# Early attention units: outputs by single heads of 64 columns, scores by pairs of heads as 256 columns

## The chip, the cores and the metric

The kernel runs on one NeuronCore of one Trainium2 chip. Its time is the device time of one execution in microseconds (us). The engines are TensorE (PE in the profile, with its weight loads as PEld), VectorE (DVE), ScalarE (ACT), GpSimd (POOL) and SyncE (SP), which issues nearly all DMAs.

## The reference

A linear attention with a decaying state, followed by a feed-forward network with softplus.

```python
# q, k, v: (4, 8, 768, 64) float32
gamma = 1.0 - 2.0 ** (-5.0 - np.arange(H))
for t in range(S):
    state = gamma * state + k[:, :, t] (outer) v[:, :, t]        # (B, H, 64, 64)
    y[:, :, t] = (1 / sqrt(64)) * q[:, :, t] @ state
x = y.transpose(0, 2, 1, 3).reshape(3072, 512)
h = x @ w_in                                                      # (512, 2048), float64
g = np.maximum(h, 0) + np.log1p(np.exp(-np.abs(h)))
out = (g @ w_out).astype(np.float32)                              # (2048, 512), float64
```

## The kernel before

**Attention in units.** The attention is cut into 48 units: for each of the 4 batches, 6 chunks of C = 128 tokens, and for each chunk two halves `hf` of 4 heads. In a unit, the scores of a head are k times q over the 128 tokens of the chunk, masked to the lower triangle; the output of a head is v times the masked scores, plus (from the second chunk of a batch on, `if c`) the state times q; and the state grows by k times v. The decay is multiplied into q and v ahead of all that (`decay`, on GpSimd). Head dimension is D = 64, so two heads (a pair, index `j` = 0 or 1 in a unit, member `par` = 0 or 1) fill 128 partitions.

**Early units.** The first WHOLE = 12 units, which are the whole first batch, are computed with plain float32 matmuls. The other 36 units use float32r operands that are split into a high and a low part; the change does not touch those. For an early unit n, the parts are:

- `operands` (L224): four transposes on TensorE (L232) bring k and q of both pairs into one PSUM tile `tp`. The evacuation is L234 (ScalarE, the upper-left 64 partitions of k), L235 (VectorE, the other 64 partitions of k) and L236 (ScalarE, q whole). k goes into `kz`, in which each head has its own 128 columns with zeros on the partitions of the other head; q goes into `qs` with both heads of a pair on the 128 partitions. There is one `kz` for all units and one half of `qs` for even and one for odd units.
- `scores_whole` (L262): four matmuls of 128 columns, one for each head, with `kz` as weights and `qs` as moving operand (L267), one copy to SBUF on ScalarE (`a`, L268) and the mask on GpSimd (L260).
- `new_state` (L297): two matmuls k times v into PSUM (L307). `stack_state` (L315) copies the state to `stw`, a block-diagonal matrix of 128x128 for each pair (L323, one half on VectorE, one on ScalarE).
- `outputs` (L331): for each pair, one matmul of the 128x128 state with q of the pair (L342, if c), and two matmuls (L345), each with 128 weight columns: v of one head beside 64 columns of zeros. The zeros stand in the tile of v, `vns[i][:, :, 1, :]`, and are written once at the start (L524). All three add up in the same 128 columns of `yp`, whose 128 partitions are the two heads. The evacuation is one copy on ScalarE to `xh` (L346) and one subtraction on VectorE to `xl` (L347), each of 128x256: the high and the low part of the input of the feed-forward network.

A float32 matmul is two instructions in the profile, each with its own weight load: L345 shows 96 of each for 48 matmuls. The chunks 0 of the batch are units 0 and 1; so 10 of the 12 early units have `if c`.

**The network.** The weights arrive as float64 in 16 slices of 128 columns of d_ff (`load_weights`, L69 and L70 on SP's queue) and are turned into two float32r parts by ScalarE, VectorE and GpSimd (`convert_weights`, L85 to L98). `hidden` is three float32r matmuls for each piece (L436 to L438: high by high, low by high, high by low) into `hp`, `softplus_1` and `softplus_2` follow on VectorE, ScalarE and GpSimd (L444 to L453), and `second` is three more matmuls (L471 to L473).

**What sets the order.** `tick` places each part of a unit at a fixed offset from 16 times its number (L394 to L398), and the loop at L546 and `stages` (L588) interleave ticks with the first steps of the network. In these first steps a scheduler orders each engine's instructions; from `starts[2]` on (L617) TensorE's order is as written. Every engine works its own queue in order. Early units take their PSUM banks from `attention_bank` (L218): `tp`, `sc` and `yp` of successive units go by turns into two banks.

Pair p of chunks (256 tokens, 4 units) must have its `xh` and `xl` before `hidden` can start on it: units 0 and 2 for the first two pieces, units 1 and 3 for the others.

## Time and profile before

| what | value |
|---|---|
| median of 3 runs | 659.26 us (658.81 to 661.81) |
| profiled execution: its time | 661.7 us |
| profiled execution: its span, first to last instruction | 660.0 us |
| TensorE busy | 648.3 us, 98% of the span |
| VectorE, ScalarE, GpSimd busy | 411.9, 366.7, 319.3 us |
| granted TensorE clock, mean | 0.997 |
| last output matmul of an early unit (L345) starts | 110.5 us |

The profile is one execution. "Busy" of a matmul counts it from its start to a modelled end, so matmuls overlap in it; the pace at which TensorE works is the distance from one start to the next. Rows of a timeline give the start, the length and the number of instructions of a run of like ones. In a row of a line's instructions the three figures are the shortest, median and longest duration in ns.

### The profile page before, as it was taken

What the parts mean: (1) busy time and instruction counts of PE and PEld (TensorE: products, weight loads), DVE (VectorE), ACT (ScalarE), POOL (GpSimd) and SP (SyncE); (2) the same over time, 40 slices, a digit from 0 to 9 for tenths busy, and PEclk for the clock granted to TensorE, in tenths of its full rate; (3) what the DMA queues carried; (4) which work ended last, traced back from release to release, by engine and by line L of the source; (5) the groups of instructions that cost most, each with busy time, mean ns of one, the idle gap of its engine ahead of it and who ended that gap; (6) DMA issues with size and microseconds to landing.
All of it is one profiled execution on the core that took longest, in us unless ns stands there. A gap on an engine that the chain in (4) does not pass through costs nothing.

```text
span 660.0 us, 11777 instructions
## 1 busy us (share of the span) xinstructions
PE 648.3 (98%) x3762; PEld 555.2 (84%) x3762; DVE 411.9 (62%) x756; ACT 366.7 (56%) x799; POOL 319.3 (48%) x330
## 2 busy tenths in 40 slices
PE   7999999999999999999999999999999999999997
PEld 6898899888888888888888888888888888888896
DVE  5777888875685576576566665676677567522221
ACT  5867876656564555556565655565565555422221
POOL 5777758564445445444543464355345543332221
PEclk9999999999999999999999999999999999999999
DMA  9898573132223241131232132131222200000000
GB/s 241 227 260 239 161 195 86 37 76 41 42 62 62 39 96 21 26 84 35 40 84 37 35 92 35 17 82 29 46 61 48 41 19 33 0 1 33 0 33 32
DMA packets 153822, 46.69 MB, mean 71 GB/s; under 512 B 140448, under 2 KB 148640, under 8 KB 153760
## 3 DMA queue, kind: packets, MB, share of 16 engines
q1 hardware_dynamic: 153312, 45.93, 29.3%
q8 instruction: 29, 0.48, 0.3%
q14 instruction: 33, 0.27, 0.1%
q10 hardware_dynamic: 448, 0.01, 0.0%
HBM read 39.60 MB, written 6.29 MB: 70 GB/s over the span
## 4 chain that ended last, share of the span: by engine, by line
PE 92%; DMA 2%; ACT 2%; POOL 1%; issue 0%; DVE 0%; SPq 0%; POOLq 0%; ACTq 0%
PE hp L436 13%; PE hp L438 13%; PE acc L471 13%; PE acc L472 13%; PE hp L437 13%; PE acc L473 13%; PE yp L355 6%; PE sc L280 3%; PE stp L307 2%; DMA win<-in_moe_w_in_dram 2%; PE yp L345 1%; PE sc L267 1%; DMA vn<-in_v_dram 1%; PE yp L342 1%; PE tp L232 0%
## 5 line engine op out<-in xcount | busy, mean ns | idle before, releaser
L453 POOL TENSOR_TENSOR gl<-sp,gh 128x512 fp32r<-128x512 f32 x96 | 129.4, 1349 | 122.5 <-ACT gh L451 118.2
L436 PE MATMUL hp<-xh,winhl 128*128 128x512 f32 (+1 forms) x448 | 166.1, 371 | 1.0 <-DVE sp L449 0.5
L438 PE MATMUL hp<-xh,winhl 128*128 128x512 f32 (+1 forms) x448 | 162.0, 362 | 0.5 <-POOL winhl L98 0.5
L437 PE MATMUL hp<-xl,winhl 128*128 128x512 f32 (+1 forms) x448 | 161.7, 361 | 0.0
L445 ACT ACTIVATE sp<-sp 128x512 f32<-128x512 f32 x96 | 60.7, 632 | 167.7 <-DVE sp L444 167.6
L471 PE MATMUL acc<-wouthl,gh 128*128 128x512 f32 x384 | 151.0, 393 | 0.0
L472 PE MATMUL acc<-wouthl,gh 128*128 128x512 f32 x384 | 150.3, 391 | 0.0
L473 PE MATMUL acc<-wouthl,gl 128*128 128x512 f32 x384 | 149.0, 390 | 0.0
L444 DVE TENSOR_SCALAR sp<-hp 128x512 uint32<-128x512 uint32 x96 | 66.3, 690 | 84.8 <-PE hp L438 62.4
L438 PEld LDWEIGHTS hp<-xh,winhl 128*128 128x128 f32 x448 | 84.5, 189 | 14.3 <-POOL winhl L98 0.9
L436 PEld LDWEIGHTS hp<-xh,winhl 128*128 128x128 f32 x448 | 84.6, 189 | 12.3 <-PE yp L345 0.7
L437 PEld LDWEIGHTS hp<-xl,winhl 128*128 128x128 f32 x448 | 84.8, 189 | 11.2
L451 ACT CAST gh<-sp 128x512 fp32r<-128x512 f32 x96 | 59.7, 621 | 52.1 <-PE acc L472 40.0
L449 DVE SCALAR_TENSOR_TENSOR sp<-hp,sp 128x512 f32<-128x512 f32 x96 | 65.2, 680 | 33.7 <-ACT sp L445 33.2
L260 POOL TENSOR_SCALAR_AFFINE_SELECT a<-a 128x512 f32<-128x512 f32 x48 | 36.6, 762 | 101.6 <-DVE a L281 97.1
L473 PEld LDWEIGHTS acc<-wouthl,gl 128*128 128x128 f32 x384 | 71.8, 188 | 15.1
L471 PEld LDWEIGHTS acc<-wouthl,gh 128*128 128x128 f32 x384 | 72.1, 188 | 12.4
L472 PEld LDWEIGHTS acc<-wouthl,gh 128*128 128x128 f32 x384 | 72.4, 189 | 12.0
L213 POOL TENSOR_TENSOR vn<-vn,vtabs 128x256 f32<-128x256 f32 x48 | 29.8, 621 | 83.6 <-DMA vn<-in_v_dram 71.8
L281 DVE TENSOR_REDUCE a<-sc 128x256 f32<-128x512 f32 x72 | 49.3, 685 | 4.3 <-PE sc L280 3.5
L292 POOL TENSOR_TENSOR al<-a,ah 128x512 fp32r<-128x512 f32 x36 | 47.9, 1331 | 3.1 <-ACT ah L291 3.1
L329 DVE TENSOR_TENSOR st<-stp,st 64x128 fp32r<-64x128 f32 x60 | 17.3, 289 | 44.8 <-ACT st L327 44.2
(94 smaller groups left out, 919.3 us busy)
## 6 DMA issues: line engine op xcount, KB each, us to landing
win<-in_moe_w_in_dram SPq DMA_DIRECT2D x16, 512.0 KB, 4.9
wout<-in_moe_w_out_dram SPq DMA_DIRECT2D x16, 512.0 KB, 4.4
vn<-in_v_dram SPq DMA_DIRECT2D x48, 128.0 KB, 2.8
out_dram<-o SPq DMA_DIRECT2D x24, 256.0 KB, 2.1
vn<-in_k_dram SPq DMA_DIRECT2D x30, 128.0 KB, 2.4
kb<-in_k_dram SPq DMA_DIRECT2D x208, 16.0 KB, 1.7
qb<-in_q_dram SPq DMA_DIRECT2D x208, 16.0 KB, 1.7
qn<-in_q_dram SPq DMA_DIRECT2D x12, 128.0 KB, 4.9
```

What stands on the lines that cost most here:

```text
L281: summed[n] = nc.vector.tensor_reduce(sums[n][:, 2 * j:2 * j + 2, :], sc.rearrange("p h t c -> p h c t"), axis=mybir.AxisListType.X, op=AL ...
L436: nc.tensor.matmul(to, lhsT=wt[:, 0, d, :], rhs=xh[:, d], start=d == 0, stop=False)
L437: nc.tensor.matmul(to, lhsT=wt[:, 0, d, :], rhs=xl[:, d], start=False, stop=False)
L438: nc.tensor.matmul(to, lhsT=wt[:, 1, d, :], rhs=xh[:, d], start=False, stop=d == ND - 1)
L444: nc.vector.tensor_scalar(sp.bitcast(U32), hps[s].bitcast(U32), 0x80000000, None, op0=ALU.bitwise_or)
L445: nc.scalar.activation(sp, sp, AF.Softplus)
L449: nc.vector.scalar_tensor_tensor(g, hps.pop(s), 0.0, g, op0=ALU.max, op1=ALU.add)
L451: nc.scalar.copy(gh, g)
L453: nc.gpsimd.tensor_tensor(gl, sps.pop(s), gh.bitcast(F32), op=ALU.subtract)
L471: nc.tensor.matmul(to, lhsT=gh[:, k, ts], rhs=wt[:, 0], start=first, stop=False)
L472: nc.tensor.matmul(to, lhsT=gh[:, k, ts], rhs=wt[:, 1], start=False, stop=False)
L473: nc.tensor.matmul(to, lhsT=gl[:, k, ts], rhs=wt[:, 0], start=False, stop=last)
```

## The change

The early units get other operands and other shapes; nothing else is touched.

- k of a pair is kept whole (`kts`, 128 partitions, one half of the tile for even and one for odd units), and q of each head stands beside zeros (`qzs`, one tile for even and one for odd units). So the 64-partition copies L234 and L235 now bring q, and the 128-partition copy L236 brings k.
- Scores: two matmuls of 256 columns, one for each pair, with k of the pair as weights and q of both heads as moving operand.
- Outputs: for each head by itself a matmul of the state (64 of its columns, if c) and one of v (64 columns, no zeros beside it). `yp` is on 64 partitions with 512 columns. It is evacuated in two halves: copy and subtraction for the even heads to partitions 0 to 63, then copy and subtraction for the odd heads to partitions 64 to 127.
- At the start the zeros of v are no longer written (three memsets on VectorE), those of `kz` (two on GpSimd) become four: two on GpSimd, two on VectorE.

In the changed kernel the v matmul is L343 (L345 before), the cast L345 (L346), the subtraction L346 (L347), and the network's lines are lower by one (L435 for L436).

```diff
-    kz = attn.tile([P, 2, NJ, C], F32, name="kz", tag="vhl", bufs=2)
-    qs = attn.tile([P, 2, NJ, C], F32, name="qs", tag="vhl", bufs=2)
+    kts = attn.tile([P, 2, NJ, C], F32, name="kts", tag="ah")
+    qzs = [attn.tile([P, 2, NJ, C], F32, name=f"qz{i}", tag="vhl", bufs=2) for i in range(2)]
...
-            qt = qs[:, n % 2]
-            nc.scalar.copy(kz[lo, 0], tp[lo, 0])
-            nc.vector.tensor_copy(kz[up, 1], tp[up, 0])
-            nc.scalar.copy(qt, tp[:, 1])
-            live[n] = [qt, rest[0], vn]
+            qz = qzs[n % 2]
+            nc.scalar.copy(qz[lo, 0], tp[lo, 1])
+            nc.vector.tensor_copy(qz[up, 1], tp[up, 1])
+            nc.scalar.copy(kts[:, n % 2], tp[:, 0])
+            live[n] = [qz, rest[0], vn]
...
-        for h in range(HH):
-            nc.tensor.matmul(sc[:, h, :], lhsT=kz[:, h % 2, h // 2, :], rhs=kq[:, h // 2, :], start=True, stop=True)
+        for j in range(NJ):
+            nc.tensor.matmul(sc[:, 2 * j:2 * j + 2, :], lhsT=kts[:, n % 2, j, :], rhs=qz[:, :, j, :], start=True, stop=True)
...
-            yp = attention_bank(n, [P, NJ, C], "yp")
-            v0 = vns[n % 3].rearrange("p h t d -> p (h t) d")
-            for j in range(NJ):
+            yp = attention_bank(n, [D, 2, NJ, C], "yp")
+            for h in range(HH):
+                j, par = divmod(h, 2)
                 if c:
-                    nc.tensor.matmul(yp[:, j], lhsT=st[:, j, :], rhs=kq[:, j, :], start=True, stop=False)
-                for par in range(2):
-                    at = 2 * (2 * j + par) - par
-                    nc.tensor.matmul(yp[:, j], lhsT=v0[:, at:at + 2, :], rhs=a[:, 2 * j + par, :], start=c == 0 and par == 0, stop=par == 1)
-            nc.scalar.copy(xh, yp)
-            nc.vector.tensor_tensor(xl, yp, xh.bitcast(F32), op=ALU.subtract)
+                    nc.tensor.matmul(yp[:, par, j], lhsT=st[:, j, par * D:(par + 1) * D], rhs=kq[:, par, j, :], start=True, stop=False)
+                nc.tensor.matmul(yp[:, par, j], lhsT=vn[:, h, :], rhs=a[:, h, :], start=c == 0, stop=True)
+            for par, own, oth in sides:
+                nc.scalar.copy(xh[own], yp[:, par])
+                nc.vector.tensor_tensor(xl[own], yp[:, par], xh[own].bitcast(F32), op=ALU.subtract)
             return
...
-    for par, own, oth in sides:
-        nc.gpsimd.memset(kz[oth, par], 0.0)
+    for qz, engine in zip(qzs, (nc.gpsimd, nc.vector)):
+        for par, own, oth in sides:
+            engine.memset(qz[oth, par], 0.0)
...
-    for vn in vns:
-        nc.vector.memset(vn[:, :, 1, :], 0.0)
```

Two places of the built programs, before and after. First TensorE where unit 2 puts out its heads and the network begins. A number behind a name tells its allocation: `yp_277` (before) and `yp_275` (after) are the outputs of unit 2, `yp_335` of unit 3 in both, `sc_296` and `sc_298` the scores of unit 3, `hp` the first hidden piece. "x2" counts matmuls. Before:

```order
L345 MATMUL yp_277<-a_237,vn2_92 128x128 x2
L342 MATMUL yp_277<-qs_87,stw0_88 128x128
L345 MATMUL yp_277<-a_237,vn2_92 128x128 x2
L436 MATMUL hp_385<-xh_82,winhl_251 128x256
L267 MATMUL sc_296<-qs_87,kz_86 128x128 x4
L437 MATMUL hp_385<-xl_83,winhl_251 128x256
```

And after:

```order
L343 MATMUL yp_275<-a_237,vn2_93 64x128
L342 MATMUL yp_275<-qz0_87,stw0_89 64x128
L343 MATMUL yp_275<-a_237,vn2_93 64x128
L342 MATMUL yp_275<-qz0_87,stw0_89 64x128
L343 MATMUL yp_275<-a_237,vn2_93 64x128
L342 MATMUL yp_275<-qz0_87,stw0_89 64x128
L343 MATMUL yp_275<-a_237,vn2_93 64x128
L267 MATMUL sc_298<-qz1_88,kts_86 128x256 x2
L307 MATMUL stp_94<-vn0_91,kn_194 128x128 x2
L342 MATMUL yp_335<-qz1_88,stw1_90 64x128
L435 MATMUL hp_387<-xh_82,winhl_249 128x256
```

The eight output matmuls of unit 2 alternate between state and v, and the scores, the state and the first output matmul of unit 3 now stand ahead of the first hidden matmul. Then ScalarE's queue around the same evacuation (`xh<-yp`). Before:

```order
L346 CAST xh_82<-yp_277 128x2x128
L236 COPY qs_87<-tp_269 128x256
L85 ACTIVATE win_207<-win_207 128x512
L323 COPY stw0_88<-stp_93 64x2x64
L97 CAST wouthl_318<-w_314 128x512
```

And after:

```order
L345 CAST xh_82<-yp_275 64x2x128
L323 COPY stw0_89<-stp_94 64x2x64
L97 CAST wouthl_318<-w_314 128x512
L85 ACTIVATE wout_206<-wout_206 128x512
L268 COPY a_297<-sc_298 128x512
L345 CAST xh_82<-yp_275 64x2x128
```

The one cast of unit 2 has become two, and four instructions stand between them, the last of them the copy of unit 3's scores.

More of the change, by code (lines that the diff above doesn't have):

```diff
@@ L262, in scores_whole @@
     def scores_whole(n):
-        kq = live[n][0]
+        qz = live[n][0]
         a = attn.tile([P, HH, C], F32, name="a")
         sc = attention_bank(n, [P, HH, C], "sc")
-        for h in range(HH):
-            nc.tensor.matmul(sc[:, h, :], lhsT=kz[:, h % 2, h // 2, :], rhs=kq[:, h // 2, :], start=True, stop=True)
+        for j in range(NJ):
+            nc.tensor.matmul(sc[:, 2 * j:2 * j + 2, :], lhsT=kts[:, n % 2, j, :], rhs=qz[:, :, j, :], start=True, stop=True)
         nc.scalar.copy(a, sc)
```

## The prediction

> **What bounds the kernel now.** I began with the page: busy time of each engine, the 40 slices, and the chain that ended last.
>
> ```profile
> PE 648.3 (98%) x3762; PEld 555.2 (84%) x3762; DVE 411.9 (62%) x756; ACT 366.7 (56%) x799; POOL 319.3 (48%) x330
> ...
> PE   7999999999999999999999999999999999999997
> ...
> PE 92%; DMA 2%; ACT 2%; POOL 1%; issue 0%; DVE 0%; SPq 0%; POOLq 0%; ACTq 0%
> ```
>
> TensorE is busy in every slice and makes up 92% of the chain. Time that TensorE needs more or less is therefore time of the kernel, unless it falls where TensorE waits anyway. So the next view is the busy time in stretches of 30 us up to 120 us, since the early units end at 110.5 us. The columns are the length of the stretch, then PE, PEld, DVE, ACT and POOL busy, then the clock, the DMA share and GB/s.
>
> ```profile
> 0.00:30.00 30.00, 24.77 (x147) 21.63 (x148) 18.63 (x47) 19.40 (x41) 18.90 (x33) 0.94 0.91 238
> 30.00:60.00 30.00, 28.11 (x207) 25.90 (x206) 21.84 (x39) 23.92 (x51) 23.86 (x36) 1.00 0.86 234
> 60.00:90.00 30.00, 29.45 (x212) 27.51 (x211) 23.89 (x43) 23.22 (x46) 20.80 (x20) 1.00 0.66 192
> 90.00:120.00 30.00, 29.79 (x198) 27.16 (x198) 25.50 (x42) 20.57 (x44) 21.26 (x21) 1.00 0.45 113
> ```
>
> TensorE idles 5.2 us in the first stretch, 1.9 in the second, and 0.6 and 0.2 in the others. VectorE and ScalarE are busy 20 to 25 us of 30: loaded, but not the bound. What TensorE waits for after the start, in the view of waits from 15 to 125 us, is this (us in all, times, longest):
>
> ```profile
> PE yp L342 <- ACT a L268: 1.5, 2, 1.0
> PE stp L307 <- POOL vn L213: 0.8, 1, 0.8
> PE sc L267 <- ACT qs L236: 0.6, 1, 0.6
> ...
> PE hp L436 <- ACT xh L346: 0.5, 1, 0.5
> ```
>
> These are single waits of about 1 us or less. So the change must be priced first by the pace of the matmuls that it removes and adds, then by these waits.
>
> **The pace of the matmuls.** The distance between starts gives it. From TensorE's timeline at 109 us (outputs of the last early unit), at 99 us (scores) and at 92 us (transposes):
>
> ```profile
> 109.49 0.61 PE L345 MATMUL yp<-a,vn 128*128 128x128 f32 x4
> 109.94 0.39 PE L342 MATMUL yp<-qs,stw 128*128 128x128 f32 x2
> ```
> ```profile
> 99.75 0.28 PE L437 MATMUL hp<-xl,winhl 128*128 128x256 f32 x1
> 99.87 0.28 PE L438 MATMUL hp<-xh,winhl 128*128 128x256 f32 x1
> 99.99 1.06 PE L267 MATMUL sc<-qs,kz 128*128 128x128 f32 x8
> ```
> ```profile
> 92.58 0.38 PE L232 MATMUL tp<-ident,kn 128*128 128x128 f32 x2
> 92.80 0.38 PE L232 MATMUL tp<-ident,qn 128*128 128x128 f32 x2
> ```
>
> Four float32 instructions in 109.94 - 109.49 = 0.45 us: 112 ns each (128 weight columns, 128 moving columns). The hidden matmuls, float32r with 256 moving columns, come every 120 ns. The transposes come every 0.22 / 2 = 0.11 us, 110 ns. The third shape is that of the later units, 64 weight columns in float32r:
>
> ```profile
> 122.89 0.39 PE L473 MATMUL acc<-wouthl,gl 128*128 128x512 f32 x1
> 123.11 0.64 PE L355 MATMUL yp<-ah,vhl 128*64 128x128 f32 x8
> 123.59 0.40 PE L355 MATMUL yp<-al,vhl 128*64 128x128 f32 x4
> 123.83 0.45 PE L436 MATMUL hp<-xh,winhl 128*128 128x512 f32 x1
> 124.11 0.40 PE L437 MATMUL hp<-xl,winhl 128*128 128x512 f32 x1
> ```
>
> Eight in 0.48 us: 60 ns each. The step from L473 to L355 gives 0.22 to 0.23 us for 512 float32r columns. So float32r moves a column in about 0.45 ns: 128 in 60, 256 in 120, 512 in 230.
>
> The question on which the change turns is what sets the 112 ns of a float32 instruction: its weight load (128 columns), or its moving columns at half the rate of float32r. No row of before shows float32 with 64 weight columns or 256 moving ones. The weight loads' durations (shortest, median, longest) in the views of three lines bear on it:
>
> ```profile
> L345 PEld LDWEIGHTS yp<-a,vn x96: 186/192/192, 10.1 to 110.4; 128*128 128x128 f32 x96
> L355 PEld LDWEIGHTS yp<-ah,vhl x288: 134/134/135, 122.9 to 582.1; 128*64 128x64 f32 x144
> L232 PEld LDWEIGHTS tp<-ident,kn x24: 138/142/230, 4.3 to 92.6; 128*128 128x128 f32 x24
> ```
>
> Half the columns shorten the load from 192 to 134 ns. The transposes' load is nearly as short, 142 ns, yet their pace is 110 and not 60. Something other than the load holds them, and what they share with the float32 matmuls and not with L355 is a float32 moving operand of 128 columns. I take it that float32 moves at about 0.85 ns a column, so that fewer weight columns gain nothing. Lower bound of an output instruction with 64 weight columns: 60 ns (L355); upper: 112 ns (L345); I take 110, by the transposes. For 256 moving float32 columns: lower 120 ns (the hidden matmul), upper 230 ns (twice the columns at half rate, as 512 float32r columns); I take 222, twice 110 and a little.
>
> The Trainium skill, page "TensorE: Matmul & The Clock Gate", sections "LDWEIGHTS (loading the stationary operand)" and "Back-to-back issue gap", says that a load costs by its number of columns and a matmul by its moving columns, and makes no difference for float32. By that rule an output instruction would cost the 60 ns of L355 and the sum would be the gain of the first rival; that the load shrinks with its columns agrees (192 to 134 ns), that the rest follows does not, by the transposes' 110 ns.
>
> **The change part by part.**
>
> *Outputs, units 2 to 11.* Removed: 6 matmuls of two instructions, 12 x 112 = 1.344 us. Added: 8 matmuls, 16 x 110 = 1.760 us. That is +0.416 us for each of 10 units, +4.2 us (bounds: 16 x 60 gives -3.8, 16 x 112 gives +4.5). The cause is that the state's and v's products no longer share 128 output columns of the array. *Units 0 and 1:* 8 instructions of 112 become 8 of 110: nothing (at 60: -0.8 for both).
>
> *Scores, 12 units.* 8 x 112 = 0.896 us become 4 x 222 = 0.888: -0.1 us in all (bounds: 4 x 120 gives -5.0, 4 x 230 gives +0.3).
>
> *Operands.* The same three copies with k and q exchanged, the same shapes: nothing. That `kz` is doubled frees a wait that no row of TensorE shows (L236 is waited for as the last of three copies, not for its buffer), so I expect no gain.
>
> *Evacuation.* One cast and one subtraction become two each. A copy costs by its columns, not its partitions:
>
> ```profile
> L346 ACT CAST xh<-yp x12: 352/370/381, 11.8 to 112.2; 128x256 fp32r<-128x256 f32 x12
> ...
> L378 ACT COPY vn<-yp x14: 363/366/367, 125.0 to 203.1; 64x256 f32<-64x256 f32 x14
> ```
> ```profile
> L347 DVE TENSOR_TENSOR xl<-yp,xh x12: 385/410/427, 12.2 to 113.7; 128x256 fp32r<-128x256 f32 x12
> ```
> ```profile
> DVE kz L235 <- ACT kz L234: 6.3, 3, 3.5
> ```
>
> So ScalarE gets 12 x 0.37 = 4.4 us more and VectorE 12 x 0.41 = 4.9 us, over about 100 us in which they have 15 to 30% free: covered by TensorE as throughput. As latency it is at least 0.37 + 0.41 = 0.8 us more for each unit, because the two engines take turns on one bank, as they already do in the operands (in the view of all waits up to 125 us, VectorE's copy L235 idles for ScalarE's L234; the change gives the outputs the same form). Behind the second cast on ScalarE stand weight conversions, behind the second subtraction on VectorE likewise; and TensorE waits for `xh` and for the bank. In the orders above, the second cast of unit 2 comes after the copy of unit 3's scores, and the first hidden matmul after unit 3's first output matmul, which waits for the same bank. Before, TensorE waited there 0.5 us (L436, row above) and 1.0 at most on L342; the scores, state and output matmul that now stand between (about 1.4 us) cover most of the longer evacuation. Bounds for the waits over all units: -1 us (a wait of L342 or L267 falls out, rows above) to 12 x 0.8 = +9.6 us (each one lands on TensorE). I take +0.8, one evacuation of 12, since of 12 units before only one made L436 wait.
>
> *Memsets and start.* Three memsets on VectorE go, two come, all before TensorE's first transposes: nothing.
>
> *Switches between 64 and 128 weight columns.* The Trainium skill, page "TensorEngine Tiling (Array Packing)", section "Key Properties", says that changing the tiling mode drains TensorE, which speaks against this change. The rows at 122.89 to 124.11 show the switch: 0.22 us into L355, no more than between two matmuls of 512 columns, and on the way back 0.28 instead of 0.23, the 0.05 by which a 128-column load outlasts a 60 ns matmul. I price it at nothing, and at 110 ns a matmul covers that load too.
>
> *Sum:* +4.2 - 0.1 + 0.8 = +4.9 us. The profiled execution took 661.7 us, 1.7 over its span of 660.0 and 2.4 over the median of 659.26. It would become 666.6; on the median, 664.2 us.
>
> **The rivals.**
>
> *The weight load was the limit* (the other side: faster). If float32 columns move as fast as float32r, the sum is -3.8 - 0.8 - 5.0 = -9.6 us, with +0.8 for the evacuation -8.8: 650.5 us. For it: 112 ns is also what a 128-column load takes when nothing covers it (60 + 0.05 us at 123.83). Against it: the transposes. It decides at about 95 ns for 128 float32 columns: with p for that, outputs and scores sum to 272 p - 26.0 us (16 instructions in 10 units, 8 in 2, 4 of double length in 12; 26.0 is what they take before). 0.10.
>
> *The first waits absorb it.* Four of the ten units, 2 to 5, are put out by 42.1 us. The chain then runs over SP's queue and a weight DMA into a wait of TensorE (rows of the chain, and of TensorE's timeline):
>
> ```profile
> 41.62 0.46 PE yp L345 x4
> 42.08 0.13 SPq L178
> 42.34 6.54 DMA win<-in_moe_w_in_dram
> ```
> ```profile
> 49.47 0.28 PE L438 MATMUL hp<-xh,winhl 128*128 128x256 f32 x1
> 50.73 0.49 PE L342 MATMUL yp<-qs,stw 128*128 128x128 f32 x2 [0.98 <-ACT a L268]
> ```
>
> If that transfer starts no later, 4 x 0.416 = 1.7 us vanish in this wait, and with no new waits +2.4 us remain: about 661.7 us, from +0.5 to +3.3. Against it: by the chain the transfer is issued behind a load (L178) that waited for an output matmul, so it would start later too. 0.24.
>
> *The evacuation becomes the wait.* If the ping-pong on the bank costs half its bound, +4.8 instead of +0.8, the sum is +8.9: 668.2 us. For it: VectorE is busy up to 25.5 of 30 us in these stretches, and each half must pass through both queues. Against it: only one such wait before. 0.11.
>
> *Each switch drains.* Counted from the changed order, about 20 bursts of 64-column matmuls, two switches each, at the 0.16 us by which an L355's duration (0.64 - 7 x 0.06 = 0.22) exceeds its pace: +6.4, 670.6 us. Rows at 123 us speak against it. 0.02.
>
> **How the numbers follow.** My forecast, +3.3 to +6.5 us, has 0.53. A measurement can tell about 0.5%, 3.3 us. Faster than that is only the first rival: 0.10. Within it lies the second: 0.24. Slower: 0.53 + 0.11 + 0.02 = 0.66. The likeliest is 664.2 us. The range leaves out the first rival and the upper part of the third: 659.5 (the second at its lower end) to 669.0 us.
>
> **What would show it.** In the changed profile: L343 and L342 with weight loads near 134 ns but starts 108 to 112 ns apart (60 would mean the first rival); L267 starts 215 to 230 ns apart (120 would); the first matmul of the later units (L355, now L354) about 5 us later than 122.9 to 123.1; ScalarE and VectorE busy 4 to 5 us longer. A view of waits in which hidden matmuls wait for L345 or L346 for more than 3 us in all would be the third rival; a wait near 50 us that is shorter than 1 us with the L354 mark less than 3 us later, the second. If L354 begins earlier than before, the pace I took for float32 is wrong.

## The result, and the profile after

The changed kernel takes 669.29 us (median of 4 runs, 669.0 to 670.1), the kernel before 659.51 us beside it (4 runs, 658.81 to 661.81). The ratio is 1.0143 (95%: 1.0121 to 1.0166), so the change costs 9.8 us by the medians and 9.4 by the ratio. The direction was forecast, the size was twice the forecast's 4.9 us, and the time lies 0.3 us above the range. The profiled execution took 669.25 us, with a span of 667.5. (One of the four runs of e16 below took 2281 us and is left out of its figures.)

The page of the changed kernel, the same lines as shown of before:

```profile
PE 654.1 (98%) x3754; PEld 554.3 (83%) x3754; DVE 416.4 (62%) x767; ACT 370.8 (56%) x811; POOL 319.0 (48%) x330
...
PE 92%; ACT 2%; DVE 2%; DMA 1%; issue 0%; ACTq 0%; DVEq 0%
```

TensorE is busy 5.8 us longer (4.1 were counted), VectorE 4.5 and ScalarE 4.1 (4.9 and 4.4). TensorE's share of the chain is what it was; it doesn't show where 9 us came from. The first output matmuls of the later units do (TensorE's timeline):

```profile
130.46 0.39 PE L472 MATMUL acc<-wouthl,gl 128*128 128x512 f32 x1
130.68 0.64 PE L354 MATMUL yp<-ah,vhl 128*64 128x128 f32 x8
```

They begin at 130.68 instead of 123.11: 7.6 us are lost before that mark, and the span is 7.5 us longer. All of it lies in the early units. Busy time in the first stretches (columns as in the prediction):

```profile
0.00:30.00 30.00, 22.26 (x126) 17.61 (x127) 19.38 (x48) 20.07 (x43) 19.01 (x33) 1.00 0.91 238
30.00:60.00 30.00, 29.22 (x193) 25.12 (x192) 23.25 (x43) 25.04 (x53) 22.93 (x34) 1.00 0.86 247
```

TensorE idles 7.7 us in the first 30 us (5.2 before), and then less than before, 0.8 instead of 1.9. So most of the loss is not visible idle time. TensorE is busy for longer than the passes account for, and the timeline shows with what. The last early unit, after:

```profile
115.55 0.39 PE L472 MATMUL acc<-wouthl,gl 128*128 128x512 f32 x1
115.86 0.43 PE L342 MATMUL yp<-qz,stw 128*64 128x128 f32 x2
116.13 0.38 PE L343 MATMUL yp<-a,vn 128*64 128x128 f32 x2
...
117.44 0.38 PE L343 MATMUL yp<-a,vn 128*64 128x128 f32 x2
117.75 0.39 PE L435 MATMUL hp<-xh,winhl 128*128 128x256 f32 x1
117.98 0.28 PE L436 MATMUL hp<-xl,winhl 128*128 128x256 f32 x1
```

The same place of before (the passes between are in the prediction):

```profile
109.05 0.39 PE L473 MATMUL acc<-wouthl,gl 128*128 128x512 f32 x1
...
110.53 0.36 PE L436 MATMUL hp<-xh,winhl 128*128 128x256 f32 x1
110.73 0.28 PE L437 MATMUL hp<-xl,winhl 128*128 128x256 f32 x1
```

Take the time from the start of the network's pass ahead of the outputs to the start of the second one behind them. Before it is 1.68 us for 12 output passes, after it is 2.43 us for 16: 0.75 us more, where the prediction has 0.42. Inside the burst the pace is the forecast one: 12 passes from 116.13 to 117.44, 109 ns each. The rest stands at the ends. From L472 to L342 it is 0.31 us instead of 0.23, the first pair takes 0.27 instead of 0.22, the first network pass begins 0.31 us after the start of the last pair, and the second 0.23 us after the first: together 0.54, where before has 0.34. So going to 64 weight columns and back costs about 0.3 us in float32. Next the scores:

```profile
106.53 1.03 PE L267 MATMUL sc<-qz,kts 128*128 128x256 f32 x4
107.21 0.58 PE L470 MATMUL acc<-wouthl,gh 128*128 128x512 f32 x1
107.63 0.39 PE L471 MATMUL acc<-wouthl,gh 128*128 128x512 f32 x1
```

From 106.53 to 107.63, less 0.23 for the network's pass, are 0.87 us for four passes of 256 columns: 217 ns each, as forecast (222).

The other suspect is the evacuation. Who waits for the subtraction L346 in the changed kernel (us, times):

```profile
L346 DVE TENSOR_TENSOR xl<-yp,xh x24: 404/417/419, 11.8 to 120.6; 64x256 fp32r<-64x256 f32 x24
...
  ACT xh L345: 1.7, 2
  PE yp L342: 1.2, 1
  PE yp L343: 1.0, 1
```

Before, the same list was empty for L347: nobody waited for the subtraction. Now TensorE's next output matmuls wait 2.2 us for it, because their bank is read out later. An example is unit 1, whose matmuls start at 14.0 us in both kernels. Before, ScalarE and VectorE had:

```profile
15.21 0.37 ACT L346 CAST xh<-yp 128x256 fp32r<-128x256 f32 x1 [0.41 <-PE yp L345]
```
```profile
16.32 0.42 DVE L347 TENSOR_TENSOR xl<-yp,xh 128x256 fp32r<-128x256 f32 x1
```

After, ScalarE and then VectorE:

```profile
15.05 0.36 ACT L345 CAST xh<-yp 64x256 fp32r<-64x256 f32 x1 [0.21 <-PE yp L343]
...
16.03 0.69 ACT L85 ACTIVATE win<-win 128x512 f32<-128x512 f32 x1
16.61 0.62 ACT L97 CAST wouthl<-w 128x512 fp32r<-128x512 f32 x1
17.25 0.36 ACT L345 CAST xh<-yp 64x256 fp32r<-64x256 f32 x1
```
```profile
16.36 0.41 DVE L346 TENSOR_TENSOR xl<-yp,xh 64x256 fp32r<-64x256 f32 x1
16.70 0.69 DVE L93 TENSOR_SCALAR wp<-win 128x512 uint32<-128x512 uint32 x1
17.49 0.70 DVE L94 SCALAR_TENSOR_TENSOR wp<-win,wp 128x512 uint32<-128x512 uint32 x1
18.22 0.42 DVE L346 TENSOR_TENSOR xl<-yp,xh 64x256 fp32r<-64x256 f32 x1
```

Before, the bank was free at 16.74; after, at 18.64. The second half adds 0.78 us of its own and stands behind two weight conversions on each engine: 1.9 us in all. Unit 2's first output matmul then waits 1.2 us.

So there are two theories. **Switches and passes:** TensorE's own time grew, by 0.75 us in a unit whose outputs stand in one burst, as those of the last unit do. **Halves:** the evacuation in two pieces makes TensorE wait. The first is worth more than 10 x 0.75 = 7.5 us of TensorE's time: eight of the ten units are put out in two bursts (one pair of passes, then seven), and with units 0 and 1 the changed kernel has 20 bursts of 64 columns, so by this count it is 10 x 0.42 + 20 x 0.30 = 10.2 us. The second can't be priced from these two kernels. A third, that the queues of weight conversions are what sets the early time, came up on the way.

### The profile page after: what moved, and what is told of

Same layout as the page of the kernel before. It is cut to its first block, busy times and chain, and to the rows that moved or that the text cites. A ratio compares the mean times of both kernels' runs of the same rounds, so it can differ in the third digit from the quotient of the medians.

```text
span 667.5 us, 11791 instructions
## 1 busy us (share of the span) xinstructions
PE 654.1 (98%) x3754; PEld 554.3 (83%) x3754; DVE 416.4 (62%) x767; ACT 370.8 (56%) x811; POOL 319.0 (48%) x330
## 4 chain that ended last, share of the span: by engine, by line
PE 92%; ACT 2%; DVE 2%; DMA 1%; issue 0%; ACTq 0%; DVEq 0%
PE hp L435 13%; PE hp L436 13%; PE acc L470 13%; PE hp L437 13%; PE acc L471 13%; PE acc L472 13%; PE yp L354 6%; PE sc L280 3%; PE stp L307 2%; PE yp L343 1%; PE yp L342 1%; PE sc L267 1%; DMA wout<-in_moe_w_out_dram 1%; DVE wp L94 0%; DVE w L95 0%
## 5 line engine op out<-in xcount | busy, mean ns | idle before, releaser
L435 PE MATMUL hp<-xh,winhl 128*128 128x512 f32 (+1 forms) x448 | 165.9, 371 | 0.3 <-ACT wp L91 0.3
L436 PE MATMUL hp<-xl,winhl 128*128 128x512 f32 (+1 forms) x448 | 162.2, 362 | 0.0
L470 PE MATMUL acc<-wouthl,gh 128*128 128x512 f32 x384 | 151.4, 394 | 0.6 <-ACT gh L450 0.6
L471 PE MATMUL acc<-wouthl,gh 128*128 128x512 f32 x384 | 150.2, 391 | 0.0
L472 PE MATMUL acc<-wouthl,gl 128*128 128x512 f32 x384 | 149.0, 390 | 0.2 <-POOL gl L452 0.2
L435 PEld LDWEIGHTS hp<-xh,winhl 128*128 128x128 f32 x448 | 84.5, 189 | 12.4 <-ACT wp L91 0.5
L436 PEld LDWEIGHTS hp<-xl,winhl 128*128 128x128 f32 x448 | 84.8, 189 | 11.9 <-issue 0.7
L472 PEld LDWEIGHTS acc<-wouthl,gl 128*128 128x128 f32 x384 | 71.9, 188 | 15.7 <-POOL gl L452 0.4
L470 PEld LDWEIGHTS acc<-wouthl,gh 128*128 128x128 f32 x384 | 72.1, 188 | 13.3 <-ACT gh L450 0.8
L471 PEld LDWEIGHTS acc<-wouthl,gh 128*128 128x128 f32 x384 | 72.4, 189 | 12.1
```

The lines of the kernel that those rows point to most:

```text
L435: nc.tensor.matmul(to, lhsT=wt[:, 0, d, :], rhs=xh[:, d], start=d == 0, stop=False)
L436: nc.tensor.matmul(to, lhsT=wt[:, 0, d, :], rhs=xl[:, d], start=False, stop=False)
L470: nc.tensor.matmul(to, lhsT=gh[:, k, ts], rhs=wt[:, 0], start=first, stop=False)
L471: nc.tensor.matmul(to, lhsT=gh[:, k, ts], rhs=wt[:, 1], start=False, stop=False)
L472: nc.tensor.matmul(to, lhsT=gl[:, k, ts], rhs=wt[:, 0], start=False, stop=last)
```

## The experiments

Ratios are against the kernel before, run beside each (its medians 659.5 to 660.9 us). "Last unit" is the change of the last early unit's outputs against before, measured as above, times 10 units. "Bursts" counts the stretches of matmuls with 64 weight columns in the early units. "Busy" and "idle" are TensorE's in the profile up to the mark, the first output matmul of the later units; for before they are 115.2 and 7.9 us, and 115.1 and 6.8 in its second profile (e1).

| run | outputs | evacuation | last unit x 10, us | bursts | busy, idle, us | median, us | ratio (95%) |
|---|---|---|---|---|---|---|---|
| e3 | 64 columns, halves of the array side by side | one piece | -0.6 | 17 | 114.1, 7.1 | 660.43 | 1.0000 (0.9986 to 1.0013) |
| e8 | state 128, v 64 columns | one piece | +2.4 | 22 | 114.5, 8.0 | 660.96 | 1.0013 (1.0001 to 1.0024) |
| e5 | 16 passes of 128 columns | one piece | +4.5 | 0 | 117.0, 6.5 | 662.26 | 1.0023 (1.0011 to 1.0036) |
| e2 | as before | halves | 0 | 0 | 115.1, 12.0 | 667.08 | 1.0104 (1.0089 to 1.0119) |
| e6 | as e3 | halves | -0.6 | 19 | 116.7, 12.3 | 668.11 | 1.0111 (1.0088 to 1.0134) |
| e4 | as changed | halves, both casts first | +7.5 | 17 | 120.5, 8.9 | 668.87 | 1.0131 (1.0114 to 1.0148) |
| changed | 16 passes of 64 columns | halves | +7.5 | 20 | 121.0, 9.6 | 669.29 | 1.0143 (1.0121 to 1.0166) |

The last unit stands for all only where each unit is put out in one burst. Busy times compare only to about 2 us, since in some of these profiles the granted clock was lower for a while: 0.66 between 15 and 20 us in before, e1, e3 and e6, which is 1.7 us of TensorE's full pace, and 0.94 in one stretch of 30 us in e2 and e6, which is 1.8.

**e1, before once more, unchanged** (one run): how far two profiles of one kernel differ.

> The kernel before once more, for a second profiled execution. The one shown took 661.7 us, 2.2 over the median of 659.5. Both theories expect about 659.5 here, with the first output matmul of the later units (L355) at about 121 us instead of 123.1; then the change's cost up to that mark is near 9.8 us and not the 7.6 that the two profiles so far show, and some 6 of it are waits. If the mark stays at 123 with a time of 661 or more, the two profiles can be compared as they are.

661.98 us; the mark of the later units is at 121.99 us, against 123.11 in the first profile. By these two, one profile's mark is good to about 1 us.

**e2, only the halves, in the kernel before.**

```diff
-            nc.scalar.copy(xh, yp)
-            nc.vector.tensor_tensor(xl, yp, xh.bitcast(F32), op=ALU.subtract)
+            for par, own, oth in sides:
+                nc.scalar.copy(xh[own], yp[own])
+                nc.vector.tensor_tensor(xl[own], yp[own], xh[own].bitcast(F32), op=ALU.subtract)
```

> The kernel before with one edit: its evacuation in two halves of 64 partitions (cast, subtraction, cast, subtraction), no matmul touched. Theory E (the waits come from the evacuation in halves): 663 to 667 us, that is 4 to 7 over before. Theory O (the waits come from the new order and the new operands): within 2 us of before, 658 to 661.5.

667.08 us, 1.0104: 6.9 us without any change of a matmul. Busy time up to the mark (121.99 and 127.06 us), of e1 and then of e2:

```profile
0.00:121.90 121.90, 115.13 (x770) 104.72 (x771) 93.10 (x172) 88.57 (x180) 86.95 (x109) 0.99 0.72 192
```
```profile
0.00:127.00 127.00, 115.05 (x770) 104.29 (x771) 97.02 (x186) 94.37 (x193) 86.66 (x110) 0.99 0.69 185
```

TensorE has the same 770 instructions and the same 115.1 us of work, and idles 12.0 us instead of 6.8. What it waits for in e2, from 15 to 132 us:

```profile
PE yp L342 <- ACT a L268: 2.8, 3, 1.4
PE yp L342 <- DVE xl L348: 1.2, 1, 1.2
...
PE sc L280 <- DVE a L281: 1.1, 1, 1.1
PE sc L267 <- ACT qs L236: 1.1, 1, 1.1
```

Only one of these waits is for the evacuation itself. The three others shown, 5.0 us, are for copies on ScalarE and VectorE, in whose queues the second halves now stand; the rows left out, 2.8 us, are for GpSimd. So the price is spread over other work. TensorE's order is hardly another: in the traces, the number of network matmuls ahead of each unit's last output matmul differs from e1's by five at most.

**e3, changed kernel, but each head's outputs on its own partitions and one evacuation.**

```diff
-            yp = attention_bank(n, [D, 2, NJ, C], "yp")
+            yp = attention_bank(n, [P, NJ, C], "yp")
...
+                own = sides[par][1]
...
+                nc.tensor.matmul(yp[own, j], lhsT=vn[:, h, :], rhs=a[:, h, :], start=c == 0, stop=True)
+            nc.scalar.copy(xh, yp)
+            nc.vector.tensor_tensor(xl, yp, xh.bitcast(F32), op=ALU.subtract)
```

> The changed kernel with the outputs of odd heads written to partitions 64 to 127 of the bank, so that one cast and one subtraction evacuate a unit; the same matmuls otherwise. Theory E: only the matmul work of 3.6 us is left, 662 to 664.5 us. Theory O: 667 to 670 us. If TensorE runs matmuls of different column halves side by side, starts less than 100 ns apart would show it and the time would be under 661 us.

660.43 us, 1.0000. The same two places of TensorE's timeline:

```profile
107.48 0.39 PE L472 MATMUL acc<-wouthl,gl 128*128 128x512 f32 x1
107.80 0.45 PE L343 MATMUL yp<-qz,stw 128*64 128x128 f32 x4
108.07 0.40 PE L344 MATMUL yp<-a,vn 128*64 128x128 f32 x4
...
108.88 0.39 PE L435 MATMUL hp<-xh,winhl 128*128 128x256 f32 x1
109.10 0.28 PE L436 MATMUL hp<-xl,winhl 128*128 128x256 f32 x1
```

Passes of even and odd heads go to different partitions and run side by side, about 54 ns each (four in 0.22 us). But the switch eats that up again: 107.48 to 109.10 are 1.62 us against 1.68 before. That holds for five of the ten units. The five others are put out in two bursts, a pair of passes and seven pairs; by the distances in the trace each takes about 0.4 us more than before, so over all units TensorE has an estimated 2 us more to do, and the kernel's time is that of before.

**e4, changed kernel with both casts ahead of both subtractions**, so that the bank passes once from ScalarE to VectorE.

```diff
             for par, own, oth in sides:
                 nc.scalar.copy(xh[own], yp[:, par])
+            for par, own, oth in sides:
                 nc.vector.tensor_tensor(xl[own], yp[:, par], xh[own].bitcast(F32), op=ALU.subtract)
```

> The changed kernel with the two casts ahead of the two subtractions, so that a unit's bank passes from ScalarE to VectorE once and not three times; the same amount of work on each engine. Theory E: part of the waits goes, 664 to 667.5 us. Theory O: no change, 668 to 670 us.

668.87 us, 1.0131. Its view of waits has no TensorE wait for the subtraction any more, and yet its interval and the changed kernel's overlap by most of their width. (One wait of 0.9 us is for a cast.) The taking of turns on the bank is not the price.

**e5, changed kernel with 128 weight columns** (zeros beside v, as before; 16 passes, no switch) and one evacuation.

```diff
-                    nc.tensor.matmul(yp[:, par, j], lhsT=st[:, j, par * D:(par + 1) * D], rhs=kq[:, par, j, :], start=True, stop=False)
-                nc.tensor.matmul(yp[:, par, j], lhsT=vn[:, h, :], rhs=a[:, h, :], start=c == 0, stop=True)
+                    nc.tensor.matmul(yp[:, j], lhsT=st[:, j, :], rhs=kq[:, par, j, :], start=par == 0, stop=False)
+                nc.tensor.matmul(yp[:, j], lhsT=v0[:, at:at + 2, :], rhs=a[:, h, :], start=c == 0 and par == 0, stop=par == 1)
...
```

> The changed kernel with its eight output matmuls of a unit, but with 128 weight columns each (the whole block-diagonal state for each head; v beside its zeros), so that they add up in 128 partitions and one cast and one subtraction evacuate them. TensorE's work is that of the change (16 instructions of 112 ns for 12), without the evacuation in halves and without 64-column weights. If that work lands in full: +4.1 us over before, 664 to 665.5. If the waits of the first 60 us absorb it: 660.5 to 663. If it costs what is left of the change beside the halves (669.3 - 667.1): 662.5 to 663.

662.26 us, 1.0023: 1.5 us. It is also the control for the switch, since it has the changed kernel's 16 passes:

```profile
109.48 0.39 PE L473 MATMUL acc<-wouthl,gl 128*128 128x512 f32 x1
109.71 0.38 PE L344 MATMUL yp<-qz,stw 128*128 128x128 f32 x2
...
111.27 0.39 PE L345 MATMUL yp<-a,vn 128*128 128x128 f32 x2
111.41 0.36 PE L436 MATMUL hp<-xh,winhl 128*128 128x256 f32 x1
111.61 0.28 PE L437 MATMUL hp<-xl,winhl 128*128 128x256 f32 x1
```

109.48 to 111.61 are 2.13 us, against 2.43 with 64 columns. The switch there and back is the 0.30. And of 10 x 0.45 = 4.5 us that the four passes more take in e5, the kernel's time shows 1.5 (0.7 to 2.4). Where the rest went is not shown: up to the mark TensorE is busy 1.9 us longer than in e1 and idles 0.3 us less, and e1's lower clock (above) lengthens e1's busy time by up to 1.7 us.

**e6, e3 with the evacuation in halves** (`xh[own]`, `yp[own]` as in e2).

> The kernel of e3 (odd heads on partitions 64 to 127, where column halves run side by side) with its evacuation in halves, two casts and two subtractions as in the change. Theory E (the halves cost by themselves): 660.4 + 6.5 = 665.5 to 668 us, though TensorE has less to do than before. If the halves cost only where TensorE is full: 660 to 663.

668.11 us, 1.0111. In the code, nothing but the halves differs from e3: 7.3 us. That is e2's price again, on other matmuls.

**e7, e9, e10, the work of the halves without their order:** the kernel before with a cast and a subtraction more for each unit, 64 x 256, into a tile that nobody reads (e7 both, e9 the cast alone, e10 the subtraction alone).

```diff
+            nc.scalar.copy(spare[lo], xh[lo].bitcast(F32))
+            nc.vector.tensor_tensor(spare[up], xl[up].bitcast(F32), xl[up].bitcast(F32), op=ALU.subtract)
```

> The kernel before, its evacuation in one piece, followed in each early unit by one cast of 64x256 on ScalarE and one subtraction of 64x256 on VectorE to a tile that nobody reads: the work of the halves without their latency. Theory W (the work itself, in the two queues, delays what stands behind it): 664.5 to 667.5 us. Theory L (only the later end of the evacuation counts: bank and input of the network): 659.5 to 662 us.

> As e7, but only the spare cast on ScalarE (12 of 0.37 us), not the subtraction. If the work of the halves costs through ScalarE's queue: near e7's 663.8, 662.5 to 664.5. If through VectorE's: no change, 659 to 661.5.

> As e7, but only the spare subtraction on VectorE (12 of 0.4 us), not the cast. If the work of the halves costs through VectorE's queue: 662.5 to 664.5. If through ScalarE's: 659 to 661.5.

663.80 us, 1.0049 (1.0033 to 1.0066) for both; 663.89, 1.0041 (1.0022 to 1.0060) for the cast; 664.92, 1.0055 (1.0034 to 1.0075) for the subtraction. The prices don't add up: one operation more on either engine costs about 3 us, both together the same. So both queues pay, where the expectations had one of the two. The spare work is not quite that of the halves. The spare cast takes 0.40 us, but the spare subtraction, from SBUF to SBUF, takes 0.42 to 1.40 us in e7 (median 0.94): 10.3 us for its twelve, against 5.0 us for the kernel's own twelve. So VectorE has twice the work of the halves, and even so the work alone costs about half of e2's price.

**e8, the kernel before with v in 64 columns** to each head's own partitions, the state's matmul as it was.

```diff
-                for par in range(2):
-                    at = 2 * (2 * j + par) - par
-                    nc.tensor.matmul(yp[:, j], lhsT=v0[:, at:at + 2, :], rhs=a[:, 2 * j + par, :], start=c == 0 and par == 0, stop=par == 1)
+                for par, own, oth in sides:
+                    nc.tensor.matmul(yp[own, j], lhsT=vn[:, 2 * j + par, :], rhs=a[:, 2 * j + par, :], start=c == 0, stop=True)
```

> The kernel before with v of each head as 64 weight columns, written to the head's own 64 partitions of the bank, in place of 128 columns with zeros; evacuation in one piece. If two column halves run side by side as in e3, the starts of the v matmuls come in pairs and TensorE needs 0.45 us less for each of 12 units. By theory E the time is set by other things where the early units are, so little comes of it: 657.5 to 661 us; if TensorE's work counted in full, 655 us.

660.96 us, 1.0013. The expectation counted passes alone. With the switches, twice in each unit here, the burst takes 1.92 us and not less than 1.68:

```profile
108.60 0.39 PE L471 MATMUL acc<-wouthl,gl 128*128 128x512 f32 x1
108.83 0.38 PE L341 MATMUL yp<-qs,stw 128*128 128x128 f32 x2
109.14 0.44 PE L343 MATMUL yp<-a,vn 128*64 128x128 f32 x4
109.51 0.49 PE L341 MATMUL yp<-qs,stw 128*128 128x128 f32 x2
...
110.52 0.28 PE L435 MATMUL hp<-xl,winhl 128*128 128x256 f32 x1
```

So e3 and e8 don't show that less work of TensorE gains nothing; over all units they had more.

**e11, the hand-offs without the work:** the kernel before, evacuated in two halves of 128 columns instead of 64 partitions. As many turns between the engines, but shorter steps:

```diff
-            nc.scalar.copy(xh, yp)
-            nc.vector.tensor_tensor(xl, yp, xh.bitcast(F32), op=ALU.subtract)
+            for j in range(NJ):
+                nc.scalar.copy(xh[:, j], yp[:, j])
+                nc.vector.tensor_tensor(xl[:, j], yp[:, j], xh[:, j].bitcast(F32), op=ALU.subtract)
```

> The kernel before with its evacuation in two steps of 128 columns on all 128 partitions (cast, subtraction, cast, subtraction) in place of two steps of 64 partitions with 256 columns. The bank passes between the engines as often as in e2, but a step has half the columns, so the work grows by about 0.15 us on each engine for a unit and not by 0.4. If the passing back and forth through two ordered queues is what costs: near e2's 667.1, 665 to 668 us. If the work is: 660.5 to 662.5 us.

```profile
L347 ACT CAST xh<-yp x24: 245/266/285, 11.9 to 117.1; 128x128 fp32r<-128x128 f32 x24
...
L348 DVE TENSOR_TENSOR xl<-yp,xh x24: 272/283/294, 12.2 to 117.7; 128x128 fp32r<-128x128 f32 x24
```

661.04 us, 1.0004 (0.9986 to 1.0023): nothing. (A half of 64 partitions takes as long as the whole: cast and subtraction take 364 and 417 ns in the changed kernel, 370 and 410 before. A half of the columns takes 266 and 283.)

**e12, e3 with the bank emptied at once** by one ScalarE copy, and the halves then made from that copy in SBUF.

```diff
-            nc.scalar.copy(xh, yp)
-            nc.vector.tensor_tensor(xl, yp, xh.bitcast(F32), op=ALU.subtract)
+            nc.scalar.copy(ys, yp4)
+            for par, own, oth in sides:
+                nc.scalar.copy(xh4[own], ys[own])
+                nc.vector.tensor_tensor(xl4[own], ys[own], xh4[own].bitcast(F32), op=ALU.subtract)
```

> The kernel of e6 with one copy of the whole bank to SBUF by ScalarE first, and the casts and subtractions in halves from there. The bank comes free after the first step of 0.37 us, while the input of the network comes later still and ScalarE has one copy of 0.37 us more for each unit. If the cost of the halves is the bank that is held: well under e6's 668.1, 661 to 664.5 us (what the work costs by e7 stays). If it is the queues or the late input: 667 to 671 us.

673.41 us, 1.0186 (1.0168 to 1.0204). One step of ScalarE hands the bank back, and the kernel is 5 us slower than with halves from the bank (e6). So the bank that is held is not the main price; how much it is can't be read here, since the copy and the slower casts give ScalarE 5.2 us more work than in e6.

**e13, e11 with e7's spare work:** hand-offs and work together, but in another form than the halves.

> The kernel before with the evacuation in two steps of 128 columns (e11) and behind it the spare cast and the spare subtraction of e7. If the cost of the halves is the work in the queues and the longer evacuation together: 665.5 to 668 us, as e2. If the work alone counts and the rest of e2 comes from something special to halves of 64 partitions: 663 to 665 us, as e7.

666.66 us, 1.0082 (1.0066 to 1.0099): 5.4 us. Work alone 3, hand-offs alone 0, together 5 to 6; the interval meets e2's (1.0089 to 1.0119). But the work is more than e2's: casts and subtractions give ScalarE 6.8 us more than before and VectorE 11.4, where e2 has 4.4 and 5.1.

**e14 and e15, e2's halves in the first six units alone, or the last six.**

```diff
-            for par, own, oth in sides:
+            for par, own, oth in sides if n < 6 else ((0, slice(0, P), None),):
```

> The kernel before with the evacuation in halves for units 0 to 5 only. If the cost arises where the chain runs through conversions and weight DMAs (the first 50 us): most of e2's 6.9, 664.5 to 667 us. If it arises later: 660 to 662.5.

> The kernel before with the evacuation in halves for units 6 to 11 only. If the cost arises in the first 50 us: 660 to 662.5 us. If it arises where VectorE is fullest (60 to 125 us): 664.5 to 667. Evenly spread: e14 and e15 both at 663 to 664.5.

663.81 us, 1.0045 (1.0028 to 1.0061), and 664.78, 1.0060 (1.0045 to 1.0075). Together 1.05%, which is e2's 1.04%. The first six units pay 3.0 us and the last six 4.0, about 0.6 us for each on average; the late units pay as well, where TensorE seemed to have cover.

**e16, scores on 64 partitions:** in the kernel before, one copy of the transposes as they are, no zeros, scores of even and odd heads into two banks with two copies behind them. It takes the copy L235 off VectorE; ScalarE gets one copy of 512 columns for L234 and L236, and two of 256 for L268.

```diff
-            nc.scalar.copy(kz[lo, 0], tp[lo, 0])
-            nc.vector.tensor_copy(kz[up, 1], tp[up, 0])
-            nc.scalar.copy(qt, tp[:, 1])
+            nc.scalar.copy(kqw[n % 2], tp)
...
+                nc.tensor.matmul(sc[:, j, :], lhsT=kw[own, 0, j, :], rhs=kw[own, 1, j, :], start=True, stop=True)
+            nc.scalar.copy(a.rearrange("p (j t) c -> p j t c", t=2)[:, :, par], sc)
```

> The kernel before with less work for ScalarE and VectorE in the early units: k and q are evacuated whole by one copy of 128x512 on ScalarE (three copies before), and the scores of a head take its own 64 partitions of both, without zeros, even heads into one bank and odd heads into another, each evacuated by one copy of 128x256. VectorE has one copy of 0.43 us less for each of 12 units, ScalarE about the same. If the time follows the work of VectorE in the early stage as in e10, but downwards: 656 to 658.5 us. If the turn of four instead of three uses of two banks makes new waits, or less work buys nothing: 659.5 to 663.

667.75 us, 1.0108 (1.0072 to 1.0143), slower than either expectation. It is no test of less work on VectorE, because TensorE changed too. Busy time up to its mark (129.16 us):

```profile
0.00:129.10 129.10, 126.57 (x770) 111.23 (x771) 88.63 (x162) 88.69 (x181) 86.01 (x107) 1.00 0.68 182
```

TensorE idles 2.5 us instead of e1's 6.8, so the waits did get shorter; but it is busy for 126.6 us instead of 115.1 with the same 770 instructions. Two reasons show in the timeline. Scores on 64 partitions are a switch as well: from L471 at 93.15 us to L470 at 94.45, around four score passes, it takes 1.30 us, where 0.23 + 4 x 0.11 + 0.23 would be 0.90, and there are 22 such bursts, most of four passes. And the float32 passes come 213 ns apart until about 30 us, in before only until 9 us and from 16.6 to 20; why is not shown.

**e17 and e18, before and changed with most of the weight conversion left out** (sign and lowest three bits of the weights).

```diff
...
-            nc.vector.scalar_tensor_tensor(wp, high, 0x80000000, wp, op0=ALU.bitwise_and, op1=ALU.bitwise_or)
-            nc.vector.scalar_tensor_tensor(w, high, 3, wp, op0=ALU.logical_shift_left, op1=ALU.bitwise_or)
+            nc.vector.tensor_scalar(w, high, 3, None, op0=ALU.logical_shift_left)
```

> The kernel before with most of the weight conversion left out: the sign and the lowest three bits of each weight are not put together, so VectorE has one step of 0.69 us for a slice of w_in and one for a slice of w_out in place of five, and ScalarE one step of 0.63 us less; 33 us less on VectorE and 10 us less on ScalarE in the early stage. Its own time is not of interest for the reference. If the conversion sets the time of the early stage: 650 to 656 us. If it does not: 659 to 661.

> The changed kernel with the same part of the weight conversion left out. If the conversion in the two queues is what the evacuation in halves delays, the difference to e17 falls from 8.8 to 9.8 us to about the matmuls' work, 2 to 5 us. If the halves cost for another reason (the bank, the late input), the difference stays at 8 to 10 us.

664.80 us, 1.0063 (1.0039 to 1.0088), and 672.12, 1.0182 (1.0151 to 1.0213). e17, in the stretches in which before had VectorE busy for 21.8 and 23.9 us and GpSimd for 23.9 and 20.8 (columns as above):

```profile
30.00:60.00 30.00, 28.95 (x211) 26.83 (x210) 19.85 (x26) 22.59 (x45) 26.87 (x36) 1.00 0.96 271
60.00:90.00 30.00, 28.24 (x201) 27.02 (x202) 20.00 (x34) 24.75 (x50) 28.82 (x27) 0.94 0.68 200
```

VectorE has less to do (up to the mark 71.9 us, against 93.1 in e1), GpSimd is all but full in the second, and the kernel is 4 us slower. So shorter conversion queues on VectorE did not give time back, and the third theory falls in that form; GpSimd's part of the conversion was not made shorter. The difference between the two kernels is 7.3 us instead of 9.4 to 9.8, between what the two theories expected.

## Why the prediction was half right

*The pace* held. Float32 passes of 64 columns come 109 ns apart (110 forecast), score passes 217 (222), and the first rival, with 60 and 120, is out. Four passes more for each unit are the +4.2 us of the sum as TensorE's time.

*"I price it at nothing"*, of the switches, failed. I read the switch from L355, which is float32r: 0 on the way in and 0.05 us on the way back. In float32 it is 0.30 us for there and back (2.13 against 2.43 us in e5 and the changed kernel, same passes). It is there in every burst: the 13 bursts of the changed kernel that no wait touches take 0.29 to 0.44 us more than their passes and neighbours at their usual pace, the last burst of e5 takes 0.04. With 20 bursts that is 6 us of TensorE's time, what the fourth rival said with 20 x 0.32, and I gave that rival 0.02. The Trainium skill, page "TensorEngine Tiling (Array Packing)", section "Key Properties", says that a change of mode drains TensorE; these rows agree with it, where I had set it aside on the strength of rows of another type.

*"I take +0.8"*, of the evacuation, failed too. In kernels with fewer passes or cheaper ones, e2 and e6, the halves cost 6.9 and 7.3 us, and TensorE's idle time grows by 4 to 5.5. In the changed kernel TensorE idles 1.7 us more than in before and 2.8 more than in e1. The bound that I wrote beside it, 12 x 0.8 = +9.6, held it; the choice of one evacuation in twelve did not. I counted how often TensorE waited for `xh` before and took the rest as covered. e14 and e15 show that the early and the late units both pay. And I looked for the price in a wait for the evacuation, when most of it shows as longer waits for other copies in the same two queues (e2). The third rival, half the bound, 668.2 us, was near the time by luck: its mechanism, the turns on the bank, isn't it. With fewer of them e4 is as slow, and with as many of them e11 costs nothing.

*That TensorE's time is the kernel's time* failed too, in the other direction. With one evacuation 4.5 us (e5) cost 1.5 and 2.4 us (e8) cost 0.9 (0.1 to 1.6): about a third. From e2 to the changed kernel TensorE gets 10.2 us of passes and switches more, and the ratio grows from 1.0104 to 1.0143, by 2.6 us: a quarter. A small slip stands beside it: the second rival's lower end, +0.5 on 659.26, is 659.8 and not 659.5.

*What stays open* is how the 9.4 us divide between passes, switches and halves. If the prices simply add up, the halves are 6.9 us and TensorE's 10.2 us the remaining 2.6; with the third of e5 and e8 for the latter it would be 6.9 + 3.4 = 10.3, more than was measured. The traces suggest another split. Up to its mark, the changed kernel (130.68 us) is 7.6 us behind before, 5.8 busy and 1.7 idle, and 7.1 us behind e5 (123.54) with equal passes:

```profile
0.00:130.60 130.60, 120.98 (x762) 103.71 (x763) 98.47 (x185) 93.35 (x194) 88.16 (x110) 1.00 0.66 180
```
```profile
0.00:123.50 123.50, 117.03 (x762) 105.72 (x763) 91.93 (x176) 88.75 (x181) 87.01 (x109) 1.00 0.71 190
```

Of these 7.1 us, 4.0 are TensorE's busy time, so the switches as far as no wait covers them, and 3.1 are idle; e2's 5.1 us behind e1 are all idle. So in the changed kernel the larger part stands in TensorE's own time, and the halves seem to cost it less than they cost e2, since they wait behind a slower TensorE. That is argued from single profiles: no run has the switches in full with one evacuation, since 64 partitions of output force two. That the halves are enough for 6.9 us in the kernel before is shown, and so is the 0.30 us of a switch; what each costs inside the changed kernel is not. Nor is it settled why work (3 us) and hand-offs (0) together cost 5 to 7. Every variant also got an order of its own for the early stage on ScalarE and VectorE; holding that fixed wasn't tried.

None of the variants beats the kernel before; e3 and e11 come level with it, e8 nearly.

## What to carry to other kernels

Where one engine is busy 98% of the time, a small operation more on the engines that feed it can still cost more than work on the busy one: in e2, 0.8 us a unit on ScalarE and VectorE cost about 0.6 us a unit of the kernel, in e5, 0.45 us a unit on TensorE about a third of itself. Price an output's layout by its evacuation: 64 partitions with 512 columns took two pieces of the full price each here. And read a switch of tile shapes from rows of the same type, from the pass ahead of a burst to the second pass behind it, and count the bursts: behind the first pair nothing shows inside one. A variant that touches matmul shapes, as e16, has to be read by TensorE's busy and idle time before it says anything of another engine.

## What the runs showed of the hardware

- Changing between 128 and 64 weight columns costs 0.30 us for there and back in float32, spread over the pass ahead, the first pair and two passes behind; in float32r about 0.05 us (L355).
- Float32 passes with 64 weight columns to different halves of the partitions run side by side, 54 ns each instead of 109 (e3). With the switch, 16 of them in one burst take 1.62 us, 12 of 128 columns 1.68.
- Changing between 128 and 64 rows (partitions of the operands) costs about 0.40 us for there and back in float32 (e16, 93.15 to 94.45 us).
- A float32 pass takes 109 ns for 128 moving columns with 64 weight columns and 109 to 112 with 128, and 217 ns for 256 moving columns with 128 weight columns.
- A cast or subtraction from PSUM takes as long for 64 partitions as for 128 (364 and 370 ns, 417 and 410 ns, 256 columns each).
